# Attention tiles in slots, weight halves between the first loads, low parts from two products and an addition

## The chip, the cores and the metric

The kernel runs on one core of a Trainium2 chip. The core has a matrix engine (TensorE, PE in the profile), two engines for elementwise work (VectorE, DVE, and ScalarE, ACT), GpSimd (POOL) and a queue that issues DMAs (SyncE, SP). The metric is the device time of one execution in microseconds. Three runs of the kernel before took 1499.41, 1500.47 and 1502.14 us; the median is 1500.47.

## The reference

```python
# q, k, v: (8, 8, 576, 64) float32
q_c = q.reshape(B, H, nc, 64, D)           # chunks of 64 tokens, k_c and v_c alike
scores = scale * np.matmul(q_c, k_c.transpose(0, 1, 2, 4, 3))
attn = np.exp(scores - max); attn = attn / (sum(attn) + 1e-9)
x = matmul(attn, v_c) -> (4608, 512)       # tokens x (heads * 64)

h = x @ w_in                               # (512, 2048), float64 weights
g = np.maximum(h, 0.0) + np.log1p(np.exp(-np.abs(h)))     # softplus
x = (g @ w_out).astype(np.float32)         # (2048, 512)

h = np.maximum(np.maximum(x @ w1, x @ w2), x @ w3)        # 512 x 768 each
return (h @ w_out2).astype(np.float32)
```

The weights arrive as float64, so the chip reads each number as two 32-bit words.

## The kernel before

**Tiling.** The 4608 tokens are nine blocks of 512, each with four attention tiles (two heads of 512 tokens). The 2048 columns of the first MLP are 16 columns `j` of 128. For block `b` and column `j`, `mlp1` runs a projection group of twelve products (line 665, into a `ph` bank), softplus on ACT, a cut into a high and a low part, and a second group of twelve products (line 685) that adds into the four `acc` banks. After the last column of a block, four results are copied from `acc` to `tmp` tiles (lines 702 to 720) and stored to DRAM in `x2d`. The second MLP begins behind all of this and is not touched.

**Two parts.** Every operand of a product is held as a high part and a low part, and a product is three passes over them (`PASS`). `x` tiles and weight halves lie in slots of 128 x 2 x 512 numbers: 32 of kind `w`, 8 of kind `x`, 4 of kind `z`, one `qh`, one `vh`. Smaller results lie in nine `tmp` tiles (line 219). A buffer names its kinds in the order in which they are tried.

**Weights.** There are 32 weight halves (16 of `w_in`, 16 of `w_out`). `conv` loads one as pairs of words and turns it into a float `a` and a rest, in six DVE instructions (lines 301 to 339). `conv1` makes the two parts. For `j` under `SUMS` it copies `a` to the high part, lets PE sum `-high + a + rest` by three products with plus or minus the identity (lines 373 to 375), and ACT casts the sum to the low part. For the later `j`, `cut_up` does it on DVE with a subtraction and an addition.

**Attention.** The first eight tiles go through `attention_first`, with slots of kind `w`. The others go through `attention`: q and k are transposed on DVE into `tmp` tiles (lines 594, 595), PE makes the scores, softmax follows on DVE and ACT, the probabilities are transposed into a `tmp` tile (line 633), written to DRAM as `pd` and read back into another `tmp` tile by four DMAs (line 642). The products with v run with the next tile's scores (line 471).

**Early weights of the second MLP.** `early` converts 24 halves from block 2 on and stores them to DRAM; their slots are of kind `z`, then `x`.

**What sets the order.** `Plan.order` replays the kernel with costs and due times and gives each engine its list. An operation that allocates takes a free place at that moment; one that finds none waits, and others go first. On the chip each engine then runs its list in order and waits by semaphores; a tile that is used again waits for its last reader, a DMA store among them. SP's list holds nearly all loads and stores; ACT issues a part of the first ones.

Of the kernel before, what the change touches and what calls it, by code (L numbers as in the profile page):

```python
# [10 lines left out]
F32 = mybir.dt.float32  # L11
# [4 lines left out]
ALU = mybir.AluOpType  # L16
# [4 lines left out]
P = 128  # L21
# [157 lines left out]
def tile_kernel(ctx: ExitStack, tc: tile.TileContext, q, k, v, w_in, w_out, w1, w2, w3, wo2, out):  # L179
    nc = tc.nc  # L180
# [83 lines left out]
    T0, STEP = 30.0, 6.0  # L264
    T1 = T0 + STEP * (NB * NJ + 1)

    SUMS = 8
    turns = [(0, 0, 4), (1, 0, 8), (0, 4, NJ), (1, 8, NJ)]
    turns += [(b, 0, NJ) for b in range(2, NB)]
    steps = [(b, j, j == lo, j == hi - 1) for b, lo, hi in turns for j in range(lo, hi)]  # L270
# [6 lines left out]
    def in_line(kind, o):  # L277
        o.follow, line[kind] = line.get(kind), o
        return o


    def conv(src, view, kinds, due=None, after=(), most=("load",), rest=None):

        raw, a, t, free = slot(*kinds, shape=[P, TB, 2], dt=I32), Buf("tmp"), Buf("tmp"), Buf(*most)
        kind, j = view

        def load(e):
            if kind == "in":
                nc.sync.dma_start(
                    out=raw.t.rearrange("p (k f) t -> p k (f t)", k=KD),  # L290
                    in_=src[:, j * 2 * P:(j + 1) * 2 * P].rearrange("(k p) f -> p k f", p=P),
                )
            else:
                nc.sync.dma_start(out=raw.t.rearrange("p f t -> p (f t)"), in_=src[j * P:(j + 1) * P, :])

        in_line("load", op({"S": 0.5}, load, w=[raw], alloc=[free, raw], after=after, lat=2.0, move=2.2))
        hw = lambda: raw.t[:, :, 1]
        lw = lambda: raw.t[:, :, 0]
        ai = lambda: a.t.bitcast(I32)
        ti = lambda: t.t.bitcast(I32)  # L300
        op(
            {"D": 0.43},
            lambda e: nc.vector.tensor_scalar(ai(), hw(), 0x7FFFFFFF, None, ALU.bitwise_and),  # L303
            r=[raw],
            w=[a],
            alloc=[a, t],
        )
        op(
            {"D": 0.43},
            lambda e: nc.vector.tensor_scalar(  # L310
                a.t, a.t, f32_of_bits(0x47EFFFFF), f32_of_bits(0x38000000), ALU.min, ALU.max
            ),
            w=[a],
        )
        op(
            {"D": 0.43},
            lambda e: nc.vector.tensor_scalar(ai(), ai(), 3, 0x3FFFFFF8, ALU.logical_shift_left, ALU.bitwise_and),
            w=[a],
        )
        op(  # L320
            {"D": 0.69},
            lambda e: nc.vector.scalar_tensor_tensor(  # L322
                ai(), hw(), -0x40000000, ai(), ALU.bitwise_and, ALU.bitwise_or
            ),
            r=[raw],
            w=[a],
        )
        op({"D": 0.43}, lambda e: nc.vector.tensor_scalar(ti(), ai(), -0x800000, None, ALU.bitwise_and), r=[a], w=[t])
        last = op(
            {"D": 0.69},  # L330
            lambda e: nc.vector.scalar_tensor_tensor(
                rest.t[:, 1] if rest else t.t, lw().bitcast(U32), 2.0**-52, t.t, ALU.mult, ALU.mult
            ),
            r=[raw, t],
            w=[(rest, "rest")] if rest else [t],
            alloc=[rest] if rest else [],
            hold=[free],
            due=due,
        )
        return a, t, last  # L340
# [12 lines left out]
    def flat(z):  # L353
        return z.t if z.place[0] == "ph" else z.t[:, 0]
# [3 lines left out]

    def conv1(key, src, view, due):
        w = wbuf[key] = slot("w")  # L360
        kw = dict(most=("load", "load0"))
        if key[1] >= SUMS:
            a, t, last = conv(src, view, ("z", "w"), **kw)
            cut_up(w, lambda: a.t, [a], alloc=[w], rest=t, due=due)
            return last

        a, t, last = conv(src, view, ("z", "w"), rest=w, **kw)
        copy_op(lambda: w.t[:, 0], lambda: a.t, [a], [(w, "h")])
        ps = Buf("ph", "aps")

        def sums(e):
            o = flat(ps)
            nc.tensor.matmul(o, eye.t[:, 1, :P], w.t[:, 0], start=True, stop=False)  # L373
            nc.tensor.matmul(o, ident, a.t, start=False, stop=False)  # L374
            nc.tensor.matmul(o, eye.t[:, 0, :P], w.t[:, 1], start=False, stop=True)

        op({"P": 1.4}, sums, r=[eye, a, (w, "h"), (w, "rest")], w=[ps], alloc=[ps])
        copy_op(lambda: w.t[:, 1], lambda: flat(ps), [ps], [(w, "l")], psum=True, due=due, engs="A", after=[last])
        return last


# [200 lines left out]
        to_x(t, pv, view)  # L582

    before = []

    def attention(t, after=()):

        if t < NTILE:
            Rq, Rk, Rv = Buf("rq"), Buf("rk"), Buf("rv")
            qT, kT = Buf("tmp"), Buf("tmp")  # L590
            loads(load_32(t, q, lambda: Rq.t), Rq, "q", 2.2, [Rq], after=after)
            loads(load_32(t, k, lambda: Rk.t), Rk, "k", 2.2, [Rk], after=after)
            loads(load_v(t, lambda: Rv.t, 0), Rv, "v", 1.6, [Rv], after=after)
            op({"D": 0.69}, lambda e: nc.vector.transpose(qT.t, Rq.t), r=[Rq], w=[qT], alloc=[qT])
            op({"D": 0.69}, lambda e: nc.vector.transpose(kT.t, Rk.t), r=[Rk], w=[kT], alloc=[kT])
        G = Buf("aps")
        old = before.pop() if before else None

        def products(e):
            if old:  # L600
                v4 = old[1].t.rearrange("p (c e d) -> p c e d", e=2, d=D)
                p4 = old[2].t.rearrange("p (a u i) -> p u a i", a=2, i=32)
                for c in range(HP):
                    for r, k in four:
                        at = slice(TB // 2 + c * CH, TB // 2 + (c + 1) * CH)
                        square(G.t[:, :, at], v4[:, c, k], p4[:, k * HP + c], r, k)
            if t < NTILE:
                scores(G, lambda: qT.t, lambda: kT.t)

        parts = [(G, "v")] * (old is not None) + [(G, "s")] * (t < NTILE)  # L610
        op(
            {"P": 0.5 * len(parts) + 0.4},
            products,
            r=(list(old[1:]) if old else []) + ([qT, kT] if t < NTILE else []),
            w=parts,
            alloc=[G],
            after=last_t[-1:],
            due=T0 + STEP * (4 * (t - 1 - HP) + 2.25),
        )
        if old:  # L620

            def view(z, flat):
                if flat:
                    return z.rearrange("p (r f) -> p r f", r=2)
                return z[:, :, TB // 2:]

            to_x(old[0], G, view)
        if t == NTILE:
            return
        pbuf = Buf("p")  # L630
        softmax(G, pbuf)
        pt, pT = Buf("tmp"), Buf("tmp")
        op({"D": 0.69}, lambda e: nc.vector.transpose(
            pt.t.rearrange("p (b u i) -> p b u i", b=2, i=32), pbuf.t.rearrange("p (u b i) -> p b u i", b=2, i=32)
        ), r=[pbuf], w=[pt], alloc=[pt])
        pd = Buf("pd")
        op({"S": 0.48}, lambda e: nc.sync.dma_start(out=pd.t, in_=pt.t), r=[pt], w=[pd], alloc=[pd], lat=2.2)
        for n in range(4):
            c, b = divmod(n, 2)
            op(  # L640
                {"S": 0.48},
                lambda e, n=n, c=c, b=b: nc.sync.dma_start(
                    out=pT.t[n * 32:(n + 1) * 32, :].rearrange("j (a f) -> j a f", a=2),
                    in_=pd.t[c * CH:(c + 1) * CH, b * (TB // 2):(b + 1) * (TB // 2)].rearrange("(a j) f -> j a f", a=2),
                ),
                r=[pd],
                w=[(pT, n)],
                alloc=[pT] if n == 0 else [],
                lat=2.2,
            )  # L650
        before.append((t, Rv, pT))


    acc_of = {}
# [78 lines left out]
    def early(n, due, after):  # L733

        if n < NJ2:
            a, t, _ = conv(wo2, ("out", n), ("z", "x"), after=after)
            z = slot("z", "x")
            cut_up(z, lambda: a.t, [a], alloc=[z], rest=t, due=due)
            store["o", n] = op({"S": 0.48}, lambda e: nc.sync.dma_start(out=wo2d[n], in_=z.t.bitcast(F32)), r=[z], lat=2.0, move=2.2)
            return  # L740
        n -= NJ2
        a, t, _ = conv((w1, w2, w3)[n // 2 % 3], ("in", n // 6 * 2 + n % 2), ("z", "x"), after=after)
        tt_op(lambda: a.t, lambda: a.t, lambda: t.t, ALU.add, [t], [a], due=due)
        store["w", n] = op({"S": 0.48}, lambda e: nc.sync.dma_start(out=w2d[n], in_=a.t), r=[a], lat=2.0, move=1.1)

# [331 lines left out]
```

## Time and profile before

| | |
|---|---|
| median of three runs | 1500.47 us |
| profiled execution | 1499.52 us |
| its span in the profile | 1497.7 us |
| PE busy | 1445.6 us, 97% |
| DVE busy | 790.6 us, 53% |
| ACT busy | 456.5 us, 30% |

The trace is of one execution. A row of the order in time has a start, a duration, the engine, the line, the operation with output and inputs, and in brackets how long the engine had been idle and what ended that. PE's matmul durations overlap, so the distance between starts tells what one costs.

### The profile page before, as it was taken

The numbers are of one execution on the slowest core, as the hardware profiler recorded it, in microseconds if no ns is written. First come the engines' busy times: TensorE is split into PE (matmuls) and PEld (weight loads), VectorE is DVE, ScalarE is ACT, GpSimd is POOL, SyncE is SP. The second block draws the span as 40 slices with busy tenths as digits, with TensorE's granted clock in tenths as the row PEclk, the third lists the DMA queues.
The fourth block names the chain that finished last, engine by engine and source line by source line (L and its number), as shares of the span: only waits on it lengthen the run. The fifth ranks groups of instructions, "written<-read, shape, count | busy, mean of one in ns | idle before, by whom it ended". The sixth has DMA issues, their size and how long they took to land.

```text
span 1497.7 us, 26084 instructions
## 1 busy us (share of the span) xinstructions
PE 1445.6 (97%) x10642; PEld 1250.0 (83%) x10642; DVE 790.6 (53%) x1562; ACT 456.5 (30%) x890; POOL 0.7 (0%) x7
## 2 busy tenths in 40 slices
PE   4999999998998998989999999999999999999998
PEld 3677878887886886868888888999999999999997
DVE  6868874564443463535455355554554545545443
ACT  2533322232222132222222343332322323323222
POOL 0000000000000000000000000000000000000000
PEclk7999999999998999999999999999999999999999
DMA  7454235644424334343232321222322223222222
GB/s 248 135 144 138 86 83 130 152 127 112 115 59 117 88 81 119 83 99 100 63 127 65 112 64 36 92 71 85 99 85 86 74 82 105 80 85 86 70 71 85
DMA packets 229080, 147.48 MB, mean 98 GB/s; under 512 B 168032, under 2 KB 196704, under 8 KB 228960
## 3 DMA queue, kind: packets, MB, share of 16 engines
q1 hardware_dynamic: 225696, 144.24, 33.4%
q8 instruction: 83, 1.36, 0.4%
q10 hardware_dynamic: 3264, 1.57, 0.4%
q14 instruction: 37, 0.30, 0.1%
HBM read 109.58 MB, written 36.18 MB: 97 GB/s over the span
## 4 chain that ended last, share of the span: by engine, by line
PE 93%; DMA 2%; DVE 1%; SPq 1%; ACT 1%; issue 1%; ACTq 0%; DVEq 0%
PE acc L685 26%; PE ph L665 25%; PE ph L835 16%; PE one L835 12%; PE acc L953 10%; PE aps L471 2%; PE acc L471 1%; DMA x2d<-tmp 1%; PE ph L374 1%; DMA s<-in_q_dram 1%; SPq L438 1%; SPq L413 1%; ACT s L254 0%; PE ph L373 0%; ACT tmp L675 0%
## 5 line engine op out<-in xcount | busy, mean ns | idle before, releaser
L685 PE MATMUL acc<-g,s 128*128 128x512 f32 x1728 | 426.6, 396 | 18.4 <-ACT tmp L254 14.4
L665 PE MATMUL ph<-s,s 128*128 128x512 f32 x1728 | 418.1, 392 | 1.4 <-ACT tmp L675 1.4
L685 PEld LDWEIGHTS acc<-g,s 128*128 128x128 f32 x1728 | 326.1, 190 | 90.3 <-ACT tmp L254 15.9
L665 PEld LDWEIGHTS ph<-s,s 128*128 128x128 f32 x1728 | 325.8, 189 | 72.1 <-ACT tmp L675 2.4
L835 PE MATMUL ph<-s,s 128*128 128x256 f32 x1944 | 267.8, 283 | 0.0
L835 PEld LDWEIGHTS ph<-s,s 128*128 128x128 f32 x1944 | 251.8, 192 | 4.1
L261 DVE TENSOR_TENSOR tmp<-one,tmp 128x256 f32<-128x256 f32 x241 | 101.9, 423 | 246.9 <-PE one L835 217.3
L261 DVE TENSOR_TENSOR g<-tmp,g 128x512 fp32r<-128x512 f32 x198 | 135.9, 687 | 167.2 <-ACT g L254 163.1
L675 ACT ACTIVATE tmp<-ph 128x512 f32<-128x512 f32 x144 | 86.0, 598 | 426.1 <-PE ph L665 218.9
L254 ACT COPY tmp<-ph 128x256 f32<-128x256 f32 x268 | 100.2, 374 | 347.5 <-PE ph L835 346.3
L835 PE MATMUL one<-s,s 128*128 128x256 f32 x1458 | 201.6, 283 | 0.0
L835 PEld LDWEIGHTS one<-s,s 128*128 128x128 f32 x1458 | 186.7, 192 | 0.2
L953 PE MATMUL acc<-s,g 128*128 128x512 f32 x648 | 157.1, 391 | 0.5 <-DMA s<-wo2d 0.5
L953 PEld LDWEIGHTS acc<-s,g 128*128 128x128 f32 x648 | 118.3, 188 | 23.3 <-DMA s<-wo2d 0.9
L254 ACT CAST g<-tmp 128x512 fp32r<-128x512 f32 x191 | 119.1, 624 | 53.9 <-PE acc L685 40.0
L261 DVE TENSOR_TENSOR tmp<-tmp,tmp 128x256 f32<-128x256 f32 (+1 forms) x152 | 83.1, 547 | 3.9
L303 DVE TENSOR_SCALAR tmp<-s 128x512 int32<-128x512 int32 x56 | 23.5, 420 | 116.3 <-PE aps L471 107.0
L254 ACT CAST s<-tmp 128x512 fp32r<-128x512 f32 (+1 forms) x103 | 61.7, 604 | 27.9 <-DVE tmp L322 14.1
L254 ACT COPY tmp<-acc 128x512 f32<-128x512 f32 x48 | 27.7, 588 | 85.8 <-PE aps L471 27.2
L261 DVE TENSOR_TENSOR s<-tmp,s 128x512 fp32r<-128x512 f32 (+1 forms) x72 | 46.3, 654 | 7.5 <-ACT s L254 6.7
L256 DVE COPY tmp<-acc 128x512 f32<-128x512 f32 x17 | 11.8, 692 | 59.9 <-ACT tmp L254 39.8
L322 DVE SCALAR_TENSOR_TENSOR tmp<-s,tmp 128x512 int32<-128x512 int32 x56 | 38.3, 683 | 0.4
(85 smaller groups left out, 694.2 us busy)
## 6 DMA issues: line engine op xcount, KB each, us to landing
s<-wo2d SPq DMA_DIRECT2D x54, 512.0 KB, 3.3
s<-in_moe_w_out_dram SPq DMA_DIRECT2D x22, 512.0 KB, 4.7
x2d<-tmp SPq DMA_DIRECT2D x36, 256.0 KB, 2.7
s<-in_moe_w_dram SPq DMA_DIRECT2D x18, 512.0 KB, 3.9
s<-x2d SPq DMA_DIRECT2D x18, 512.0 KB, 4.8
s<-in_moe_w_in_dram SPq DMA_DIRECT2D x16, 512.0 KB, 5.0
out_dram<-tmp SPq DMA_DIRECT2D x29, 256.0 KB, 4.5
pd<-tmp SPq DMA_DIRECT2D x28, 256.0 KB, 2.0
```

Of the source, the lines that this page charges most:

```text
L254: nc.scalar.copy(dst(), src())
L261: return op({"D": 0.69 * n}, lambda e: nc.vector.tensor_tensor(dst(), a(), b(), f), r=r, w=w, **kw)
L303: lambda e: nc.vector.tensor_scalar(ai(), hw(), 0x7FFFFFFF, None, ALU.bitwise_and),
L322: lambda e: nc.vector.scalar_tensor_tensor(ai(), hw(), -0x40000000, ai(), ALU.bitwise_and, ALU.bitwise_or),
L374: nc.tensor.matmul(o, ident, a.t, start=False, stop=False)
L413: dma(out=dst().rearrange("p (g i) -> p g i", i=32)[a * 32:(a + 1) * 32, o // 32:(o + n) // 32, :], in_=src[b, t % HP * 2 + h, s:s + n, ha ...
L471: nc.tensor.matmul(dst[ROWS[k], r], w[ROWS[r]], x[ROWS[r]], start=True, stop=True)
L665: nc.tensor.matmul(ph.t, w[:, wi, kk * P:(kk + 1) * P], x[kk].t[:, xi], start=(kk == 0 and wi == 0 and xi == 0), stop=(kk == KD - 1 and wi ...
L675: in_line("y", op({"A": 0.6}, lambda e: nc.scalar.activation(l.t, ph.t, AF.Softplus), r=[ph], w=[l], alloc=[l]))
L685: nc.tensor.matmul(acc[m // 2].t[:, m % 2], w[:, wi, m * P:(m + 1) * P], g.t[:, gi, :], start=(first and wi == 0 and gi == 0), stop=(last ...
L835: nc.tensor.matmul(dst(), ws.t[:, wi, col + kk * P:col + (kk + 1) * P], x.t[:, xi, kk * HT:(kk + 1) * HT], start=(first and kk == 0 and wi ...
L953: nc.tensor.matmul(acc[t // 2].t[:, t % 2], g.t[:, gi, t * P:(t + 1) * P], wo.t[:, wi], start=(j == 0 and wi == 0 and gi == 0), stop=(j == ...
```

## The change

Four edits. The transposed q and k of an attention tile lie in the two halves of one slot (`qh`, then `z`), and the two tiles of transposed probabilities in another (`vh`, then `z`), in place of four `tmp` tiles. The first four weight halves get due times of their own for their loads (-70, -59, -55, -51), so that they stand between the first loads of q, k and v. `SUMS` is 16, so all 32 halves take the way over PE; PE now sums `rest - high` in two products, and DVE adds `a` while it writes the low part. `early` tries `x` before `z`, and raw weights of `j` from 12 on may only lie in `z`.

```diff
-    SUMS = 8
+    SUMS = 16
...
-        in_line("load", op({"S": 0.5}, load, w=[raw], alloc=[free, raw], after=after, lat=2.0, move=2.2))
+        in_line("load", op({"S": 0.5}, load, w=[raw], alloc=[free, raw], after=after, lat=2.0, move=2.2, due=first))
...
         w = wbuf[key] = slot("w")
-        kw = dict(most=("load", "load0"))
+        n = 2 * key[1] + key[2]
+        kw = dict(most=("load", "load0"), first=(-70.0, -59.0, -55.0, -51.0)[n] if n < 4 else None)
...
-        a, t, last = conv(src, view, ("z", "w"), rest=w, **kw)
+        a, t, last = conv(src, view, ("z", "w") if key[1] < 12 else ("z",), rest=w, **kw)
         copy_op(lambda: w.t[:, 0], lambda: a.t, [a], [(w, "h")])
         ps = Buf("ph", "aps")
 
         def sums(e):
             o = flat(ps)
-            nc.tensor.matmul(o, eye.t[:, 1, :P], w.t[:, 0], start=True, stop=False)
-            nc.tensor.matmul(o, ident, a.t, start=False, stop=False)
-            nc.tensor.matmul(o, eye.t[:, 0, :P], w.t[:, 1], start=False, stop=True)
-
-        op({"P": 1.4}, sums, r=[eye, a, (w, "h"), (w, "rest")], w=[ps], alloc=[ps])
-        copy_op(lambda: w.t[:, 1], lambda: flat(ps), [ps], [(w, "l")], psum=True, due=due, engs="A", after=[last])
+            nc.tensor.matmul(o, eye.t[:, 0, :P], w.t[:, 1], start=True, stop=False)
+            nc.tensor.matmul(o, eye.t[:, 1, :P], w.t[:, 0], start=False, stop=True)
+
+        op({"P": 0.5}, sums, r=[eye, (w, "h"), (w, "rest")], w=[ps], alloc=[ps])
+        tt_op(lambda: w.t[:, 1], lambda: flat(ps), lambda: a.t, ALU.add, [ps, a], [(w, "l")], due=due, after=[last])
...
-            qT, kT = Buf("tmp"), Buf("tmp")
+            QK = slot("qh", "z", dt=F32)
+            qT, kT = half(QK, 0), half(QK, 1)
...
-        pt, pT = Buf("tmp"), Buf("tmp")
+        PT = slot("vh", "z", dt=F32)
+        pt, pT = half(PT, 0), half(PT, 1)
...
-            a, t, _ = conv(wo2, ("out", n), ("z", "x"), after=after)
-            z = slot("z", "x")
+            a, t, _ = conv(wo2, ("out", n), ("x", "z"), after=after)
+            z = slot("x", "z")
...
-        a, t, _ = conv((w1, w2, w3)[n // 2 % 3], ("in", n // 6 * 2 + n % 2), ("z", "x"), after=after)
+        a, t, _ = conv((w1, w2, w3)[n // 2 % 3], ("in", n // 6 * 2 + n % 2), ("x", "z"), after=after)
```

The edits move instructions, because the order is planned from them. First ACT's list at the end of block 3 before: `ph` is a projection's bank, `acc` the banks of the second products, `g` their input, and the number behind `tmp` is the tile.

```order
L675 ACTIVATE tmp_75<-ph_90 128x512 [waits DVE_49,DMAHW2_49,PE_49,Activation_49]
L254 CAST g_74<-tmp_75 128x512 [waits Activation_49]
L254 COPY tmp_75<-acc_93 128x512 [waits DVE_49,PE_49]
L254 COPY tmp_75<-acc_93 128x512 [waits DMAHW0_49,Activation_49]
L254 COPY tmp_75<-acc_92 128x512 [waits DMAHW4_49,DMAHW3_49,DMAHW5_49,DMAHW2_49,DMAHW6_49,PE_49,Activation_49]
L675 ACTIVATE tmp_80<-ph_89 128x512 [waits PE_49]
```

The same place on ACT now (lines are two further down):

```order
L677 ACTIVATE tmp_82<-ph_90 128x512 [waits PE_49]
L254 CAST g_74<-tmp_82 128x512 [waits Activation_49]
L254 COPY tmp_78<-acc_93 128x512 [waits PE_49]
L254 COPY tmp_80<-acc_93 128x512 [waits DMAHW3_49]
L254 COPY tmp_75<-acc_92 128x512 [waits PE_49]
L254 COPY tmp_81<-acc_92 128x512
L677 ACTIVATE tmp_79<-ph_89 128x512 [waits DVE_49,PE_49]
```

Three of the copies went to one tile, the fourth to DVE; now four go to four tiles.

SP's list at the same block end before: `x2d` is the store of the copied results, `pd_87` the probabilities that are read back, `rv` the next v.

```order
L719 DMA x2d_123<-tmp_75 128x512 [waits DMAHW0_49,Activation_49]
L289 DMA s_125_4360<-in_moe_w_dram 128x4x256 [waits DMAHW1_49]
L719 DMA x2d_123<-tmp_75 128x512 [waits DMAHW2_49,Activation_49]
L642 DMA tmp_75<-pd_87 32x2x256 [waits DMAHW3_49,DMAHW2_49,PE_49]
L642 DMA tmp_75<-pd_87 32x2x256 [waits DMAHW4_49]
L642 DMA tmp_75<-pd_87 32x2x256 [waits DMAHW5_49,PE_49]
L642 DMA tmp_75<-pd_87 32x2x256 [waits DMAHW6_49]
L438 DMA rv_85<-in_v_dram 64x4x64 [waits DMAHW7_49,PE_49]
```

And now on SP:

```order
L645 DMA s_154_4314<-pd_87 32x2x256 [waits DMAHW7_49,DMAHW5_49]
L645 DMA s_154_4314<-pd_87 32x2x256 [waits DMAHW6_49]
L645 DMA s_154_4314<-pd_87 32x2x256
L645 DMA s_154_4314<-pd_87 32x2x256 [waits DMAHW0_49]
L289 DMA s_155_4356<-in_moe_w_dram 128x4x256 [waits DMAHW1_49,PE_49]
L413 DMA rk_84<-in_k_dram 32x4x32 [waits DMAHW2_49]
L413 DMA rk_84<-in_k_dram 32x4x32 [waits DMAHW3_49]
L721 DMA x2d_123<-tmp_78 128x512 [waits DMAHW4_49,Activation_49]
L721 DMA x2d_123<-tmp_80 128x512 [waits DMAHW5_49,Activation_49]
```

The four loads of probabilities stood behind two stores, and stand ahead of all four now.

PE's list up to the first projection product of the kernel before: `s_10` holds plus and minus the identity, `s_23`, `s_24`, `s_35` and `s_40` are the first block's `x`.

```order
L471 MATMUL acc_93<-s_39_777,s_28_555 64x64 [waits Activation_49]
L471 MATMUL acc_93<-s_39_777,s_28_555 64x64 x15
L373 MATMUL ph_89<-s_38_749,s_10_199 128x512
L374 MATMUL ph_89<-tmp_78,ident 128x512
L375 MATMUL ph_89<-s_38_749,s_10_199 128x512 [waits DVE_49]
L665 MATMUL ph_90<-s_23_502,s_13_262 128x512 x3
```

The same place on PE now: `s_4` is the identities, `s_22` holds q and k of the second block's first tile.

```order
L374 MATMUL ph_89<-s_40_713,s_4_191 128x512 [waits DVE_49]
L375 MATMUL ph_89<-s_40_713,s_4_191 128x512 [waits Activation_49]
L471 MATMUL acc_93<-ident,s_22_348 64x64 [waits DMAHW2_49,DMAHW1_49]
L471 MATMUL acc_93<-ident,s_22_348 64x64 x15
L471 MATMUL acc_93<-ident,s_22_348 64x64 [waits DMAHW4_49,DMAHW3_49]
L471 MATMUL acc_93<-ident,s_22_348 64x64 x15
L667 MATMUL ph_90<-s_33_532,s_15_235 128x512 x3
```

In both lists this sum is the fifth. Two turns of the second block's q and k with their scores came ahead of the projection before; one turn does now.

## Rows read from the trace of the kernel before

**Rows 1.** The page, first part: busy us, share of the span, instructions.

```profile
PE 1445.6 (97%) x10642; PEld 1250.0 (83%) x10642; DVE 790.6 (53%) x1562; ACT 456.5 (30%) x890; POOL 0.7 (0%) x7
```

**Rows 2.** Stretches: length, busy us (instructions) by engine, granted clock, DMA share, GB/s.

```profile
0.00:51.33 51.33, 30.18 (x852) 22.49 (x853) 32.74 (x73) 17.68 (x31) 0.74 (x7) 0.80 0.68 204
193.90:200.53 6.63, 4.60 (x14) 3.34 (x12) 6.63 (x14) 1.22 (x2) 0.00 (x0) 0.74 0.16 41
275.34:362.26 86.92, 86.92 (x617) 71.36 (x616) 49.25 (x91) 23.00 (x39) 0.00 (x0) 1.00 0.51 123
362.26:391.71 29.45, 25.08 (x161) 20.02 (x160) 13.43 (x23) 8.38 (x14) 0.00 (x0) 0.94 0.47 135
440.59:493.33 52.74, 46.96 (x309) 38.25 (x308) 20.11 (x37) 13.26 (x22) 0.00 (x0) 0.90 0.40 105
565.76:594.97 29.21, 22.57 (x149) 17.94 (x148) 12.04 (x22) 7.76 (x13) 0.00 (x0) 0.94 0.47 124
664.62:682.29 17.67, 11.91 (x102) 9.38 (x101) 10.71 (x19) 6.37 (x11) 0.00 (x0) 0.81 0.49 139
```

**Rows 3.** Order in time, 352 to 376: the end of block 2.

```profile
366.25 3.50 SPq L719 DMA_DIRECT2D x2d<-tmp  x4
...
368.82 0.59 ACT L254 COPY tmp<-acc 128x512 f32<-128x512 f32 x1 [1.73 <-DMA x2d<-tmp]
...
369.46 1.99 PE L685 MATMUL acc<-g,s 128*128 128x512 f32 x6 [3.35 <-ACT tmp L254]
...
371.25 4.21 PE L665 MATMUL ph<-s,s 128*128 128x512 f32 x12
```

**Rows 4.** Order in time, 448 to 478: the end of block 3.

```profile
463.65 0.59 ACT L254 COPY tmp<-acc 128x512 f32<-128x512 f32 x1 [4.92 <-DMA x2d<-tmp]
...
466.65 1.74 SPq L642 DMA_DIRECT2D tmp<-pd  x4
...
469.22 0.44 PE L471 MATMUL aps<-tmp,rv 64*64 64x64 f32 x2 [5.08 <-DMA tmp<-pd]
...
471.98 5.08 PE L685 MATMUL acc<-g,s 128*128 128x512 f32 x12
```

**Rows 5.** PE in order of time, 340 to 880: two more block ends.

```profile
575.52 2.93 PE L685 MATMUL acc<-g,s 128*128 128x512 f32 x6 [4.28 <-ACT tmp L254]
...
766.67 3.02 PE L685 MATMUL acc<-g,s 128*128 128x512 f32 x12 [0.29 <-ACT tmp L254]
```

**Rows 6.** PE in order of time, 0 to 200: a sum, and two groups.

```profile
116.95 0.40 PE L373 MATMUL ph<-s,s 128*128 128x512 f32 x1
...
118.28 2.91 PE L665 MATMUL ph<-s,s 128*128 128x512 f32 x12
...
131.89 2.88 PE L665 MATMUL ph<-s,s 128*128 128x512 f32 x12
134.61 2.88 PE L685 MATMUL acc<-g,s 128*128 128x512 f32 x12
```

**Rows 7.** Groups by line and form: busy us, mean ns, idle before.

```profile
L261 DVE TENSOR_TENSOR s<-aps,s 128x512 fp32r<-128x512 f32 x32 | 21.7, 677 | 1.3 <-ACT s L254 1.3
...
L254 ACT CAST s<-ph 128x512 fp32r<-128x512 f32 x14 | 8.2, 586 | 18.3 <-PE ph L375 15.9 <-DMA rq<-in_q_dram 2.0
```

**Rows 8.** ACT and DVE in order of time, 0 to 112: gaps in the front.

```profile
14.26 0.59 ACT L254 COPY s<-acc 128x512 f32<-128x512 f32 x1 [12.25 <-DMA s<-in_v_dram]
...
14.88 0.69 DVE L256 COPY s<-acc 128x512 f32<-128x512 f32 x1 [6.29 <-ACT s L254]
...
46.85 0.69 DVE L256 COPY s<-aps 128x512 f32<-128x512 f32 x1 [4.86 <-ACT s L254]
...
101.85 0.43 DVE L256 CAST g<-tmp 128x512 fp32r<-128x512 f32 x1 [6.11 <-ACT tmp L675]
```

**Rows 9.** PE in order of time, 0 to 200: the first projection group.

```profile
51.33 2.92 PE L665 MATMUL ph<-s,s 128*128 128x512 f32 x12
```

**Rows 10.** Who waited for whom: us in total, times, longest.

```profile
PE ph L373 <- ACT s L254: 2.4, 2, 1.2
```

More of the change, by code (lines that the diff above doesn't have):

```diff
@@ L279, in in_line, with conv @@
         return o
-    def conv(src, view, kinds, due=None, after=(), most=("load",), rest=None):
+    def conv(src, view, kinds, due=None, after=(), most=("load",), rest=None, first=None):
         raw, a, t, free = slot(*kinds, shape=[P, TB, 2], dt=I32), Buf("tmp"), Buf("tmp"), Buf(*most)
@@ L584, in tile_kernel @@
     before = []
+    half = lambda z, n: (lambda: z.t[:, n])
     def attention(t, after=()):
@@ L593, in attention @@
             loads(load_v(t, lambda: Rv.t, 0), Rv, "v", 1.6, [Rv], after=after)
-            op({"D": 0.69}, lambda e: nc.vector.transpose(qT.t, Rq.t), r=[Rq], w=[qT], alloc=[qT])
-            op({"D": 0.69}, lambda e: nc.vector.transpose(kT.t, Rk.t), r=[Rk], w=[kT], alloc=[kT])
+            op({"D": 0.69}, lambda e: nc.vector.transpose(qT(), Rq.t), r=[Rq], w=[(QK, "q")], alloc=[QK])
+            op({"D": 0.69}, lambda e: nc.vector.transpose(kT(), Rk.t), r=[Rk], w=[(QK, "k")])
         G = Buf("aps")
@@ L601, in products @@
                 v4 = old[1].t.rearrange("p (c e d) -> p c e d", e=2, d=D)
-                p4 = old[2].t.rearrange("p (a u i) -> p u a i", a=2, i=32)
+                p4 = old[2].t[:, 1].rearrange("p (a u i) -> p u a i", a=2, i=32)
                 for c in range(HP):
@@ L607, in products @@
             if t < NTILE:
-                scores(G, lambda: qT.t, lambda: kT.t)
+                scores(G, qT, kT)
         parts = [(G, "v")] * (old is not None) + [(G, "s")] * (t < NTILE)
@@ L613, in attention @@
             products,
-            r=(list(old[1:]) if old else []) + ([qT, kT] if t < NTILE else []),
+            r=([old[1]] + [(old[2], n) for n in range(4)] if old else []) + ([(QK, "q"), (QK, "k")] if t < NTILE else []),
             w=parts,
@@ L631, in attention @@
         softmax(G, pbuf)
-        pt, pT = Buf("tmp"), Buf("tmp")
+        PT = slot("vh", "z", dt=F32)
+        pt, pT = half(PT, 0), half(PT, 1)
         op({"D": 0.69}, lambda e: nc.vector.transpose(
-            pt.t.rearrange("p (b u i) -> p b u i", b=2, i=32), pbuf.t.rearrange("p (u b i) -> p b u i", b=2, i=32)
-        ), r=[pbuf], w=[pt], alloc=[pt])
+            pt().rearrange("p (b u i) -> p b u i", b=2, i=32), pbuf.t.rearrange("p (u b i) -> p b u i", b=2, i=32)
+        ), r=[pbuf], w=[(PT, "pt")], alloc=[PT])
         pd = Buf("pd")
-        op({"S": 0.48}, lambda e: nc.sync.dma_start(out=pd.t, in_=pt.t), r=[pt], w=[pd], alloc=[pd], lat=2.2)
+        op({"S": 0.48}, lambda e: nc.sync.dma_start(out=pd.t, in_=pt()), r=[(PT, "pt")], w=[pd], alloc=[pd], lat=2.2)
         for n in range(4):
@@ L642, in attention @@
                 lambda e, n=n, c=c, b=b: nc.sync.dma_start(
-                    out=pT.t[n * 32:(n + 1) * 32, :].rearrange("j (a f) -> j a f", a=2),
+                    out=pT()[n * 32:(n + 1) * 32, :].rearrange("j (a f) -> j a f", a=2),
                     in_=pd.t[c * CH:(c + 1) * CH, b * (TB // 2):(b + 1) * (TB // 2)].rearrange("(a j) f -> j a f", a=2),
@@ L646, in attention @@
                 r=[pd],
-                w=[(pT, n)],
-                alloc=[pT] if n == 0 else [],
+                w=[(PT, n)],
                 lat=2.2,
             )
-        before.append((t, Rv, pT))
+        before.append((t, Rv, PT))
     acc_of = {}
```

## The prediction

> **What bounds the kernel now.** I read the page's first part, then a table of stretches, then the order in time around the places where TensorE stands still. TensorE (PE) is busy for 97% of the span, VectorE (DVE) for 53%, ScalarE (ACT) for 30% [rows 1]. So the time is the work on PE plus the places where it waits, and a change gains only what it takes from one of these two.
>
> The waits are few. In the clean stretch from 275.34 to 362.26 PE is busy for all of 86.92 us at full clock [rows 2]. A projection group of twelve products takes 2.72 us (131.89 to 134.61 [rows 6]). The stretch holds 30 such groups and four attention pieces of 64 small products, so a piece costs (86.92 - 81.60) / 4 = 1.33 us. With these two prices the other stretches of rows 2 give what is lost at the ends of four token blocks; the groups follow from the instruction counts (161 is 64 + 8 x 12 and one more):
> 362.26 to 391.71: 29.45 - (8 x 2.72 + 1.33) = 6.36 us.
> 440.59 to 493.33: 52.74 - (15 x 2.72 + 2 x 1.33) = 9.28 us.
> 565.76 to 594.97: 29.21 - (7 x 2.72 + 1.33) = 8.84 us.
> 664.62 to 682.29: 17.67 - (3 x 2.72 + 1.33) = 8.18 us.
> Together 32.7 us. Part of it is the clock: it is granted at 0.81 to 0.94 there, and a group that follows a gap takes 4.21 or 5.08 us instead of 2.88 [rows 3, 4].
>
> The cause is a shortage of the nine `tmp` tiles. At 368.82 ACT's copy of a result from `acc` has waited until the store `x2d<-tmp` of its predecessor landed, and PE's next group waited 3.35 us for that copy [rows 3]. Before's order shows why: three of the four copies of a block end write the same tile, each behind the store of the one before. At 463.65 the copy waited 4.92 us for such a store. SP is in order, so the four loads of the transposed probabilities, issued at 466.65, stood behind a store that waited for this copy, and PE waited 5.08 us for them [rows 4]. The wait of 4.28 us at 575.52 is of the first kind [rows 5].
>
> The front has another limit. Until 51.33, the first projection product, PE is busy for 30.18 us at clock 0.80 [rows 2, 9], and DVE works through a chain with two long gaps: 6.29 us before 14.88 and 4.86 before 46.85 [rows 8].
>
> **The change part by part.**
> *Slots for the attention.* Four uses of `tmp` (q and k transposed, probabilities before and after the trip through DRAM) move to two slots, in `qh`, `vh` or `z`. The DVE and DMA instructions stay the same and cost nothing new. What goes is the reuse: after's order has four different tiles for the four copies, and no store before them in SP's queue waits for a copy that itself waits for a store. The block end at 766 shows what is left then, since before's order already has different tiles there: PE waits 0.29 us [rows 5]. ACT's four copies (2.4 us) lie under the group and the attention piece that PE runs between (2.72 + 1.33). Gain: 32.7 - 4 x 0.3 = 31.5 us. What is late next is ACT's softplus of the following column, with some 2 us to spare. Bounds: the two ends whose first wait was for `tmp<-pd` may keep theirs (18.1 us, if SP is late for another reason), or all 32.7 go.
>
> *The early block conversions* take slots of `x` before `z`. The next block's tiles also need `x`; nothing in the trace prices a wait for it. By the nearest rows it would be from zero to one gap of a block end, 9.3 us. I take zero: PE is the bound there, DVE was busy 49 of 87 us [rows 2], and after's order has the attention piece after every eighth group without exception.
>
> *Sums.* Before, a sum on PE takes 118.28 - 116.95 = 1.33 us, since the product with an unsplit fp32 operand costs several times the others [rows 6]. After, it is two products of 0.227 (2.72 / 12), 0.45 us. Now 32 halves of weights go this way rather than 16: 21.3 us of PE become 14.5. But in both orders five sums stand ahead of the first projection product, where PE isn't the bound. Behind it there are 11 x 1.33 = 14.6 before and 27 x 0.45 = 12.2 after: -2.4 us.
> On DVE each of the first 16 halves gains one addition that reads PSUM, 0.68 us by the like additions in rows 7 (10.8 us together), and each of the later 16 loses one subtraction of the same length. ACT loses 16 casts of 0.59 [rows 7], work off the path.
> Whether DVE's extra 10.8 us show depends on who leads. I counted both orders with the trace's durations. DVE's work up to the last `x` tile of the first block is 35.5 us before and 33.7 after; up to that of the second block 69.8 and 72.4. PE's work between the first products of these two blocks is 35.0 and 36.5. So at the second block DVE is later by (72.4 - 33.7) - (69.8 - 35.5) = 4.4, of which PE has 1.5 to fill. Beyond it the shares turn: at the last weights, where PE waited for DVE before and lost 6.63 - 2.72 = 3.9 us [rows 2], DVE has some 16 us in hand by the same count.
>
> The Trainium skill speaks against this part: "VectorE: DVE Perf Modes", Specifications, has ScalarE as the engine nearer to PSUM and VectorE as the one nearer to SBUF, and the change takes PSUM reads from ACT to DVE. The trace agrees in size (0.59 against 0.68 us). By the rule, with DVE as the bound, the front would be longer by the whole 10.8 us; that is the first rival.
>
> *Loads.* Four weight halves (0.5 MB each) go between the first q, k and v. Before, ACT issued loads until it could start its first copy at 14.26, waiting 12.25 us [rows 8]. In after's order ACT issues the same twelve loads, and the data ahead of its last one is about as much (three weight halves come in, most of v falls behind), so I keep 14 to 16 us. DVE gets a second half to convert in its gap of 6.29: I take 2 us less idle. If the v loads are late instead, the first tile starts up to 4 us later (1.5 MB more at the 204 GB/s of this stretch [rows 2] would be 7 us, half of it under DVE's conversions).
> *Waits of the sums themselves.* A sum can stop PE where its inputs come late. Before, the 16 sums did so twice, for 2.4 us [rows 10]; for 27 I take 27 / 16 x 2.4 = 4.1, with bounds of 0 and the 10.8 us above.
>
> Sum of the front: -2.4 (sums) - 3.9 (the wait at 196) - 2 (loads) + 2.9 (second block) + 4.1 = -1.3 us. Bounds: -8.3 (only the gains) and +10.8.
>
> **Sum.** 1497.7 - 31.5 - 1.3 = 1464.9 us of span. The profiled execution took 1499.52, 1.8 more than its span, and the median of the runs is 0.95 above it: 1464.9 + 1.8 + 0.95 = 1468 us. From the last attention piece on, PE's order is the same in both kernels, and its time stays.
>
> **Rivals.**
> *VectorE bounds the front.* For it: it is busy 32.74 of the first 51.33 us, with gaps only where others wait [rows 2, 8]. Against: the later halves return the work, and it idled 6.11 us before 101.85 until ACT's softplus came [rows 8]. Time: 1468 + 1.3 + 10.8 = 1480. Chance 0.11.
> *SP, not `tmp`, holds the probabilities.* The loads of v behind them wait for PE, and SP is in order. The ends at 469 and 566 keep their losses: 1468 + 18 = 1486. Against it: after's order has those loads ahead of the block's stores. Chance 0.09.
> *Slower: sums hold the PSUM banks.* `ph` has two banks, shared by projections and sums. Before, ACT, which is idle 70% of the time, emptied them; after, DVE does, behind up to a whole conversion (with the addition seven instructions of 0.43 or 0.69 us, as those in rows 8, some 3.8 us). Each of 27 sums that holds PE for more than (31.5 + 1.3) / 27 = 1.2 us makes the kernel slower; at 1.5 us it is 1468 + 40 = 1508. Against it: between a sum and the next projection into its bank there is mostly a group of 2.72 us. Chance 0.05.
> *No effect*: the stalls come back with other tiles, 1500. Chance 0.03.
>
> **How the numbers follow.** The forecast, 1461 to 1475 by its own terms, has 0.72. The range 1457 to 1488 takes in the first two rivals and leaves out the last two and the tails. Faster by over 0.2% (3 us, about what a measurement of this kernel can tell from no change): 0.92; within it 0.03; slower 0.05.
>
> **What would show it.** In the changed kernel PE should have no wait for ACT's copies of over 1 us at the block ends, none for the probabilities, a clock of 1.0 from some 60 us on, and 92 us for each block of 16 columns. The first projection product should start between 48 and 54 us. A first product past 58, or PE waiting for DVE again and again between 55 and 200, speaks for the first or third rival. I would be wrong altogether if PE waited at a block's first projection for a tile of `x`.

## The result and the profile after

The changed kernel takes 1463.03 us (median of 4 runs, 1461.89 to 1463.24), the kernel before 1499.94 beside it (1498.55 to 1502.14): a ratio of 0.9751, 95% interval 0.9734 to 0.9768. The forecast was 1468 in a range of 1457 to 1488. The profiled run has a span of 1461.2 us, 36.5 less than before.

The first part of the page after (busy us, share of the span, instructions), against [rows 1]:

```profile
PE 1430.9 (98%) x10642; PEld 1245.2 (85%) x10642; DVE 786.1 (54%) x1551; ACT 454.2 (31%) x885; POOL 0.7 (0%) x7
```

Stretches of the changed kernel, with the columns of [rows 2]; the last one runs from the attention piece at 290.40 to the last piece:

```profile
0.00:45.64 45.64, 25.86 (x715) 20.48 (x715) 32.76 (x73) 15.21 (x26) 0.73 (x7) 0.89 0.77 230
193.90:200.53 6.63, 6.63 (x89) 5.34 (x88) 3.58 (x7) 1.80 (x3) 0.00 (x0) 1.00 0.72 190
261.66:290.40 28.74, 24.75 (x161) 20.11 (x161) 19.89 (x37) 7.33 (x12) 0.00 (x0) 0.94 0.60 153
290.40:798.16 507.76, 507.76 (x3521) 417.33 (x3520) 251.96 (x460) 146.81 (x242) 0.00 (x0) 1.00 0.39 101
```

And the same stretch of the kernel before:

```profile
298.47:834.82 536.35, 512.91 (x3498) 419.10 (x3497) 253.67 (x466) 140.86 (x234) 0.00 (x0) 0.98 0.36 95
```

In the changed kernel TensorE is busy for all of 507.76 us, at full clock; its 22 attention pieces come every 23.08 us, which is eight groups and a piece, 8 x 2.72 + 1.33. The stretch of before holds 23 instructions fewer, which is two groups of 2.72 us (24, with one record missing). Without waits it would take 507.76 - 5.44 = 502.32 us, so it lost 34.0.

The end of block 2 after, in order of time on ScalarE; it answers to [rows 3]:

```profile
355.67 1.07 ACT L254 COPY tmp<-acc 128x512 f32<-128x512 f32 x2
357.03 1.07 ACT L254 COPY tmp<-acc 128x512 f32<-128x512 f32 x2 [0.28 <-PE acc L687]
359.75 0.60 ACT L677 ACTIVATE tmp<-ph 128x512 f32<-128x512 f32 x1 [1.64 <-PE ph L667]
```

Four copies in two pairs, and the only thing they wait for is TensorE.

One wait is new. In order of time on VectorE and TensorE, at the end of block 1:

```profile
264.12 0.43 DVE L303 TENSOR_SCALAR tmp<-s 128x512 int32<-128x512 int32 x1 [4.65 <-DMA s<-in_moe_w_out_dram]
264.46 0.68 DVE L261 TENSOR_TENSOR g<-tmp,g 128x512 fp32r<-128x512 f32 x1
265.06 0.42 DVE L310 TENSOR_SCALAR tmp<-tmp 128x512 f32<-128x512 f32 x1
265.40 2.47 DVE L261 TENSOR_TENSOR tmp<-acc,tmp 128x512 f32<-128x512 f32 x4
...
266.82 4.57 PE L687 MATMUL acc<-g,s 128*128 128x512 f32 x12 [3.99 <-DVE tmp L261]
```

VectorE works its list in order. It stands 4.65 us for the load of the first early weight, which SP issued at 259.50, and behind that conversion stand the four additions of the parked partial sums, which TensorE needs before it may write the next block's `acc`. The stretch is 28.74 us instead of 23.08: 5.66 lost, 3.99 as a wait and the rest at the lower clock after it (4.57 us for a group of 2.88). A second profile of the same kernel (a2_after_again below) has 2.86 us of this wait and 4.53 lost.

Where the 36.5 us are: 5.7 ahead of the first projection product (45.64 against 51.33 [rows 9]), 2.6 between it and 290 without the new wait, less 5.7 by the new wait, 34.0 behind, and -0.2 after the last piece. The 2.6 is what is left: the place that has as much work behind it as 298.47 of before is 290.40 + 5.44 = 295.84, which is 2.63 us earlier, and -5.69 + 5.66 - 2.6 gives that. The 5.7 is not all gain, since less work stands ahead of the product (715 instructions against 852 in the first stretches): 128 small products of the second block's q and k stand behind it now, and 128 of them take 2.0 us there (49.09 to 51.07).

### The profile page after: what moved, and what is told of

It reads as the page before. It is cut to its first block, busy times and chain, and to the rows that moved or that the text cites. A ratio compares the mean times of both kernels' runs of the same rounds, so it can differ in the third digit from the quotient of the medians.

```text
span 1461.2 us, 25970 instructions
## 1 busy us (share of the span) xinstructions
PE 1430.9 (98%) x10642; PEld 1245.2 (85%) x10642; DVE 786.1 (54%) x1551; ACT 454.2 (31%) x885; POOL 0.7 (0%) x7
## 4 chain that ended last, share of the span: by engine, by line
PE 96%; DMA 2%; DVE 1%; ACT 0%; issue 0%; SPq 0%; ACTq 0%; DVEq 0%
PE acc L687 27%; PE ph L667 27%; PE ph L837 16%; PE one L837 12%; PE acc L955 10%; PE aps L471 2%; PE acc L471 1%; DMA s<-in_moe_w_out_dram 1%; PE ph L374 1%; PE ph L375 0%; ACT s L254 0%; DMA s<-in_k_dram 0%; DMA pd<-s 0%; DMA s<-wo2d 0%; DVE tmp L261 0%
## 5 line engine op out<-in xcount | busy, mean ns | idle before, releaser
L687 PE MATMUL acc<-g,s 128*128 128x512 f32 x1728 | 420.8, 393 | 4.0 <-DVE tmp L261 4.0
L596 DVE STREAM_TRANSPOSE s<-rq 128x512 f32<-128x512 f32 x28 | 19.9, 710 | 64.7 <-PE aps L471 45.8
```

The source lines that it names most:

```text
L596: op({"D": 0.69}, lambda e: nc.vector.transpose(qT(), Rq.t), r=[Rq], w=[(QK, "q")], alloc=[QK])
L687: nc.tensor.matmul(acc[m // 2].t[:, m % 2], w[:, wi, m * P:(m + 1) * P], g.t[:, gi, :], start=(first and wi == 0 and gi == 0), stop=(last ...
```

## Experiments

**The slots alone.** The kernel before, with `attention` alone taken from the changed one:

```diff
-            qT, kT = Buf("tmp"), Buf("tmp")
+            QK = slot("qh", "z", dt=F32)
+            qT, kT = half(QK, 0), half(QK, 1)
-        pt, pT = Buf("tmp"), Buf("tmp")
+        PT = slot("vh", "z", dt=F32)
+        pt, pT = half(PT, 0), half(PT, 1)
```

> The kernel before with one part of the change alone: the attention's transposed tiles lie in slots (sums, loads, early conversions as before). Tile theory: the four block ends lost 32.7 us because nine tmp tiles were shared by the attention and the accumulator copies; with the attention out of them the four copies of a block end find four tiles, no wait of TensorE for a ScalarE copy above 1 us is left after 300 us, and the time is 1464 to 1472 us. Rival, the order theory: the waits went because the sixteen sums and the earlier loads moved the copies and the stores, so slots alone give less than half, 1480 to 1497 us.

Measured 1466.5 us, ratio 0.9785 (0.9763 to 0.9807). Its stretches:

```profile
264.01:292.74 28.73, 24.75 (x162) 20.13 (x161) 19.71 (x37) 7.33 (x12) 0.00 (x0) 0.94 0.61 163
292.74:800.50 507.76, 507.76 (x3521) 417.23 (x3520) 253.40 (x462) 146.56 (x242) 0.00 (x0) 1.00 0.39 101
```

The slots alone take away the whole loss behind 290 us, and they are enough to bring the new wait at the end of block 1. The order theory falls.

**Everything but the slots.** The changed kernel with `attention` of before and `SUMS = 8`.

> The changed kernel without the slots: the attention's transposed tiles are back in the nine tmp tiles, and the sums cover eight columns as before (in their new form); the first loads and the early conversions stay as changed. Tile theory: the block ends lose 25 to 37 us again, with copies of one block end that share a tile, and the time is 1485 to 1498 us. Order theory: the block ends stay quiet, under 1472 us.

Measured 1483.11 us, 0.9894 (0.9875 to 0.9914), a little under the expected 1485. TensorE's waits in it (us in all, times, longest):

```profile
PE acc L685 <- ACT tmp L254: 12.0, 4, 4.4
...
PE aps L471 <- DMA tmp<-pd: 5.1, 2, 4.7
```

And the stretch from 288.08 to its last piece:

```profile
288.08:818.29 530.21, 509.80 (x3497) 417.10 (x3496) 254.33 (x469) 139.10 (x232) 0.00 (x0) 0.99 0.37 96
```

530.21 - 502.32 = 27.9 us lost, inside the 25 to 37 expected, with the two kinds of wait of [rows 3, 4].

**The copies in slots, the attention left alone.** The kernel before, but at the ends of blocks 2 to 8 the four copies go elsewhere:

```diff
+            if b >= 2:
+                if m % 2 == 0:
+                    both = slot("qh", "vh", "x", dt=F32)
+                at = lambda both=both, m=m: both.t[:, m % 2]
...
+                continue
             o = Buf("tmp")
```

> The kernel before, its attention left in the nine tmp tiles as it was, but the four accumulator copies at the ends of blocks 2 to 8 go into halves of two slots that lie free there. Tile theory: whichever user leaves the nine tiles, the shortage goes; no copy waits for a store, the losses of 32.7 us go, 1464 to 1475 us. Rival, the probabilities theory: what TensorE waited for at a block's end was the attention's chain through SP's queue, which holds its tile loads in order whatever the copies do; then at least half of the loss stays, 1482 to 1500 us.

Measured 1467.44 us, 0.9791 (0.9772 to 0.981). The attention goes through `tmp`, DRAM and SP's queue as before, and yet the losses go:

```profile
297.85:804.29 506.44, 503.32 (x3498) 412.71 (x3497) 250.44 (x462) 142.71 (x239) 0.00 (x0) 1.00 0.39 101
```

Only 506.44 - 502.32 = 4.1 us stay, most of them ten waits of 0.30 or 0.35 us for ScalarE's softplus. Copies and attention took the same tiles from each other; whichever goes, the waits go. The probabilities theory (my second rival) falls.

**Five tiles instead of nine.** `mem("tmp", 9, ...)` becomes `mem("tmp", 5, ...)` in the changed kernel.

> The changed kernel with five tmp tiles instead of nine. The attention took up to four of the nine before, so five is what it left. Count theory: five tiles run as short as nine did with the attention among them, block ends lose about 30 us, 1488 to 1500 us. Holding theory: it was not the count, but that the attention's tiles are held across the way to DRAM and back (pd) and across SP's queue; with users that hold a tile for 1 to 3 us, five do nearly as well as nine, 1461 to 1472 us.

Measured 1468.0 us, 0.9795 (0.9777 to 0.9814). Around the end of block 2 it loses 1.5 us, and from 387.61 on nothing is lost:

```profile
187.00:250.24 63.24, 58.11 (x367) 46.09 (x365) 39.54 (x74) 17.98 (x30) 0.00 (x0) 1.00 0.45 109
387.61:803.04 415.43, 415.43 (x2881) 341.36 (x2880) 202.24 (x372) 115.90 (x191) 0.00 (x0) 1.00 0.35 93
```

18 pieces in 415.43 us are 23.08 each. It pays ahead of that, 5.1 us of it as waits of TensorE in 187 to 250, where the weights' conversions want two tiles each. It pays more than the 5 us by which the kernel is slower, because the new wait at block 1's end isn't in this run. So five tiles are enough for the later block ends once the attention is out.

That does not speak against a shortage in number, because the attention left fewer than five. The expectation took it to hold up to four of the nine; the trace of before shows more. Each of the 28 attention tiles there transposes q once and k once and has one group of scores, all in the same order, so counting tells which belongs to which (VectorE and TensorE: the 13th q, and the 10th and the 13th scores):

```profile
343.14 0.71 DVE L594 STREAM_TRANSPOSE tmp<-rq 128x512 f32<-128x512 f32 x1 [6.03 <-DMA rk<-in_k_dram]
...
362.78 0.65 PE L471 MATMUL aps<-tmp,tmp 64*64 64x64 f32 x32
...
441.11 0.65 PE L471 MATMUL aps<-tmp,tmp 64*64 64x64 f32 x32
```

The q transposed at 343.14 is held until 441.11, 98 us. When the copies of block 2 wait at 366, 13 q and 13 k have been transposed and the scores of 10 tiles have run: six of the nine `tmp` tiles are held. It is eight (17, 17 and 13) at 463, five at 570 and six at 668, the other ends that lose over 6 us, and four at 766, where 0.35 us was lost. The probabilities held a tile too, for 10.5 us at a time (SP and TensorE):

```profile
311.06 0.32 SPq L642 DMA_DIRECT2D tmp<-pd  x1
...
321.55 0.69 PE L471 MATMUL aps<-tmp,rv 64*64 64x64 f32 x32
```

So the attention ran several tiles ahead and left one to four for everything else. How many are held does not decide alone: in the run without slots an end with six (749 us) lost 0.35. No run varied the holding by itself, or tried more than nine tiles.

**Eight and twelve columns of sums.** `SUMS = 8` and `SUMS = 12` in the changed kernel.

> The changed kernel with the sums on TensorE for eight columns of weights instead of sixteen (two products and one addition each, as changed). If the front gained its 9.5 us by the new form of the sums and the loads, eight columns do as well: 1459 to 1465 us, with the sums' 16 x 0.45 us gone from TensorE and the same 16 products' worth of VectorE work back. If the gain came from taking VectorE work away in columns 8 to 15 (the wait of 3.9 us at 196 us of the kernel before), that wait is back: 1466 to 1470 us.

> The changed kernel with sums on TensorE for twelve columns of weights instead of sixteen. TensorE saves 8 x 0.45 = 3.6 us. Theory: VectorE takes the work of eight halves back without making TensorE wait more than 1 us in all, 1458 to 1461 us. Rival: waits for VectorE return as they did with eight columns (2.5 and 3.3 us at 178 and 188 us), and it comes out even, 1461 to 1465 us.

Measured 1460.37 us with eight (0.9735, 0.971 to 0.976) and 1463.19 with twelve (0.9758, 0.9736 to 0.978). The three intervals overlap: the number of columns can't be told apart by time. Twelve misses the 1458 to 1461 of its theory and falls to its rival: TensorE waits 3.14 us for VectorE at 189.41. Eight, in order of time on TensorE:

```profile
177.71 4.38 PE L687 MATMUL acc<-g,s 128*128 128x512 f32 x11 [2.46 <-DVE g L261]
...
188.34 4.38 PE L687 MATMUL acc<-g,s 128*128 128x512 f32 x11 [3.31 <-DVE g L261]
```

With eight, TensorE waits for VectorE again, though its time is no worse: the 16 sums that it leaves out (7.2 us of TensorE) about pay for them. Waits came back, as the second theory said, but its time of 1466 to 1470 didn't.

**The old form of the sums.** All sixteen columns with three products and a copy:

```diff
-            nc.tensor.matmul(o, eye.t[:, 0, :P], w.t[:, 1], start=True, stop=False)
-            nc.tensor.matmul(o, eye.t[:, 1, :P], w.t[:, 0], start=False, stop=True)
+            nc.tensor.matmul(o, eye.t[:, 1, :P], w.t[:, 0], start=True, stop=False)
+            nc.tensor.matmul(o, ident, a.t, start=False, stop=False)
+            nc.tensor.matmul(o, eye.t[:, 0, :P], w.t[:, 1], start=False, stop=True)
...
-        tt_op(lambda: w.t[:, 1], lambda: flat(ps), lambda: a.t, ALU.add, [ps, a], [(w, "l")], due=due, after=[last])
+        copy_op(lambda: w.t[:, 1], lambda: flat(ps), [ps], [(w, "l")], psum=True, due=due, engs="A", after=[last])
```

> The changed kernel with the old form of the sums for all sixteen columns: three products (one of them on whole fp32 numbers) and a ScalarE copy in place of two products and a VectorE addition. Price theory: a sum costs TensorE 1.33 us instead of 0.45 us, 27 of the 32 stand behind the first projection product, so about 24 us more on a TensorE that is never idle there, less some VectorE time: 1478 to 1490 us. Rival: the sums lie in waits that TensorE has anyway in the first 200 us, under 1470 us.

Measured 1484.8 us, 0.9905 (0.9884 to 0.9926): 21.8 more than the changed kernel, near the 24 expected. A sum in the old form, in order of time on TensorE:

```profile
108.56 0.40 PE L374 MATMUL ph<-s,s 128*128 128x512 f32 x1
108.80 1.02 PE L375 MATMUL ph<-tmp,ident 128*128 128x512 f32 x2
109.26 0.80 PE L376 MATMUL ph<-s,s 128*128 128x512 f32 x1
109.89 2.91 PE L668 MATMUL ph<-s,s 128*128 128x512 f32 x12
```

And one in the new form, from the changed kernel:

```profile
99.81 0.39 PE L374 MATMUL ph<-s,s 128*128 128x512 f32 x1
100.03 0.39 PE L375 MATMUL ph<-s,s 128*128 128x512 f32 x1
100.26 2.88 PE L667 MATMUL ph<-s,s 128*128 128x512 f32 x12
```

1.33 us against 0.45, or 27 x 0.88 = 23.8 us behind the first projection product, and the price is paid in full, since TensorE hardly waits there. That the time came so near the 24 expected is in part luck: here the first projection product comes 1.6 us later (47.28), and the new wait at block 1's end, 5.7 us in the changed kernel, isn't there. Moving the third term of the sum to VectorE was right even though VectorE reads PSUM for it.

**Without the early loads.** `first=None` in place of the four due times.

> The changed kernel without the due times that put four weight halves between the first loads of q, k and v; all else as changed. Loads theory (the prediction's): they bring the front 2 us, so 1464 to 1466 us here, the first projection product 1 to 3 us later than 45.64 us. Rival: they are the whole of the front's gain, then the first projection product comes at 48.5 us or later and the time is 1466 to 1470 us. Other rival: VectorE, busy with conversions it gets sooner, is what the first columns wait for anyway, and nothing changes, 1462 to 1464 us.

Measured 1460.84 us, 0.9747 (0.9727 to 0.9768): not slower. The first projection product does come later:

```profile
49.41 3.02 PE L667 MATMUL ph<-s,s 128*128 128x512 f32 x12
```

That is 3.8 us after the changed kernel's, but with 872 instructions ahead of it instead of 715. At the piece near 239 us only 1.0 is left of it (239.60 against 238.58), and then the planner's other order happens to shrink the new wait: the pieces that start at 262.68, 309.38 and 333.52 take 0.54, 1.06 and 0.66 us longer than 23.08, 2.3 in all against 5.66. The expected mechanism was seen at 45 us and not in the time.

**The early conversions' slots.** `("z", "x")` again in place of `("x", "z")`.

> The changed kernel with the early conversions taking a z slot before an x slot, as in the kernel before. The prediction put this edit at nothing (bound 0 to 9.3 us): 1461 to 1465 us, attention pieces 23.08 us apart. Rival: z slots that the transposed tiles now share with the conversions run short, and pieces after 290 us stand apart by more than 24 us: 1467 to 1473 us.

Measured 1462.66 us, 0.9758 (0.9738 to 0.9777), with the changed kernel at 1462.87 beside it: nothing, as the prediction had it.

**The additions first.** The changed kernel with two dependences more, where `adds[4:]` are block 1's four additions:

```diff
-            alloc=[a, t],
+            alloc=[a, t], after=behind,
...
-        a, t, _ = conv(wo2, ("out", n), ("x", "z"), after=after)
+        a, t, _ = conv(wo2, ("out", n), ("x", "z"), after=after, behind=() if n else adds[4:])
...
-            op({"D": 0.69}, lambda e: nc.vector.transpose(qT(), Rq.t), r=[Rq], w=[(QK, "q")], alloc=[QK])
-            op({"D": 0.69}, lambda e: nc.vector.transpose(qT(), Rq.t), r=[Rq], w=[(QK, "q")], alloc=[QK])
+            op({"D": 0.69}, lambda e: nc.vector.transpose(qT(), Rq.t), r=[Rq], w=[(QK, "q")], alloc=[QK], after=adds[4:] if t == 13 else ())
```

> The changed kernel with two added dependences: the first conversion step of the first early weight, and the transposes of one q, k tile, come behind the four additions of block 1's parked partial sums on VectorE. Queue theory: the one wait left after 60 us (3.99 us at 266.82, a stretch of 28.74 us instead of 23.08) is VectorE standing for a weight's load with the additions behind it; with the additions ahead it goes, 1456.5 to 1459.5 us. Rival, the drain theory: a block's last accumulator is free only some 4 us after its last product whatever VectorE does first, and the wait stays or another takes its place (tile of x, probabilities), 1461 to 1465 us.

> The kernel with the additions ahead once more, on one chip with the changed kernel. If the wait at block 1's end was worth its stretch, the difference to the changed kernel is -0.25 to -0.5% here too (5.4 us at 1457.6 against 1463.0 us, read on two chips); if that was the difference of two chips, it is under 0.1%.

> The changed kernel itself, for comparison on one chip: 1461 to 1465 us.

Measured 1457.59 us (0.9726, 0.9706 to 0.9747), and beside the changed kernel on one chip 1456.59 (1455.16 to 1459.35) against 1462.87 (1462.68 to 1463.35): the runs don't overlap, and the medians differ by 0.43%. In order of time on VectorE and TensorE in the run of this pair:

```profile
256.05 2.48 DVE L261 TENSOR_TENSOR tmp<-acc,tmp 128x512 f32<-128x512 f32 x4
256.68 5.60 PE L667 MATMUL ph<-s,s 128*128 128x512 f32 x24
...
259.07 0.38 DVE L303 TENSOR_SCALAR tmp<-s 128x512 int32<-128x512 int32 x1
...
263.30 3.02 PE L687 MATMUL acc<-g,s 128*128 128x512 f32 x12
```

And the stretch after the block's end, between two pieces:

```profile
262.21:282.57 20.36, 20.36 (x149) 16.71 (x149) 14.82 (x29) 5.99 (x10) 0.00 (x0) 1.00 0.51 128
```

The additions run while TensorE works on two projection groups, and the group that needs them doesn't wait: 20.36 us is seven groups and a piece, 7 x 2.72 + 1.33. The queue theory holds, and this version beats both kernels. Not all of the difference is the wait's, though. The spans of the two profiled runs of the pair differ by 7.7 us. 4.5 of it is the stretch at block 1's end in a2 (262.67 to 290.28, 27.61 us instead of 23.08). The other 3.2 lie ahead of the piece at 239.59 (236.41 here), where TensorE's rows come in the same order in both.

## Why the prediction was right, and where it was off

*Block ends* (31.5 us forecast). Right in place and cause; 34.0 came. The residual of 0.3 at each end isn't there, and before also lost 0.4 in each of two stretches between the ends (from 524.57 and 620.77) and 0.35 at 766. "A shortage of the nine tiles" has to be put more exactly: at the four ends five to eight of them lay with q and k transposed far ahead, and five would do once the attention is out.

*"What is late next".* This step failed. I named ScalarE's softplus, and looked for new waits only at the ends of blocks 2 and later. What came was VectorE's wait for a weight at the end of block 1, 5.7 us. With the slots the planner puts a conversion ahead of the four additions, and its load came at 264.12, after TensorE had run out of other work at about 262.8. How much that costs goes with the order: TensorE waits 3.98 us with the slots alone, 2.45 with twelve columns, 0.47 without the early loads, and not at all with the old sums or five tiles.

*Sums.* The price of 0.45 us was right. "The waits of the sums themselves" (+4.1) was too dear: behind the first projection product one of 0.78 us came. The two waits of [rows 10] from which it was scaled lie at 33.60 and 43.48, ahead of that product, and did not belong in a count of what comes behind it. The second block's lag (+2.9) was 1.4: from the first projection product of the first block to that of the second it is 37.79 us after (45.64 to 83.43) and 36.36 before (51.33 to 87.69). The second one after:

```profile
83.43 8.38 PE L667 MATMUL ph<-s,s 128*128 128x512 f32 x36
```

And before:

```profile
87.69 5.60 PE L665 MATMUL ph<-s,s 128*128 128x512 f32 x24
```

The mechanism of this lag was wrong as well: VectorE was to be the late one, but TensorE is busy for 37.39 of the 37.79 us. The lag is TensorE's own work, the 128 small products more, and near the 1.5 us of the forecast's count for TensorE. That 1.4 already holds the sums of this stretch, three before and six after, which -2.4 counts too (3 x 1.33 - 6 x 0.45 = 1.3). Counted once, -2.4 + 1.3 - 3.9 + 1.4 + 0.8 is -2.8 for what lies behind the first projection product; the trace has -2.6. The wait of 3.9 at 196 went, but more than one part can take it away: with the slots alone it is down to 0.65 us, at 192.05; with the slots and the new sums in eight columns such waits are back (2.46 and 3.31), and sixteen columns take them off.

*Loads* (-2). Without them the first projection product comes 3.8 us later, the piece at 239 us 1.0 later, and the whole kernel takes no more time. That product came at 45.64, outside the 48 to 54 I had named; the forecast left out that less work stands ahead of it.

*Sum.* 1464.9 us of span were forecast and 1461.2 came: the front and the block ends together gained 9.4 us more than I had, and the new wait took 5.7 back. The 3.7 us between them are the difference of two larger errors, so that the number came this close is luck; that the block ends give most of it is not.

*Rivals.* VectorE didn't bound the front: between 55 and 200 us TensorE waited for it twice, for 0.8 and 0.5 us, and the granted clock was 1.00 from 50 us on until the new wait. The Trainium skill ("VectorE: DVE Perf Modes", Specifications) has VectorE as the engine farther from PSUM. The trace agrees in sign: the same copy out of `acc` takes 0.69 us on VectorE and 0.59 on ScalarE [rows 8]. VectorE had the time, so nothing came of it here. The slower rival (sums that hold PSUM banks) would have shown as waits of TensorE for VectorE's additions at the sums or at the projections behind them; these two of 0.8 and 0.5 us are all there are behind the first projection product.

## What to carry to other kernels

Where copies wait for the stores of their predecessors, ask who else holds tiles of that pool, how many at once and for how long: here one user had run ahead and held up to eight of nine. Moving either user out took all or nearly all of the loss, and five tiles were enough for the others from block 3 on. More tiles were not tried. After a stall is taken out, go through each in-order engine of the new order for an instruction that waits for a load and has an accumulator's reader behind it. A stall can cost more than its wait: 3.99 us of waiting cost 5.66 here, since the clock was low for the group after it, while with twelve columns 2.45 us at the same place cost 2.51 and the group after it took 3.00.

## What was not expected of the hardware

The clock in the front differs from run to run. The kernel with the slots alone and the kernel before run the same groups up to there, but the first projection product came at 48.85 in one and 51.33 in the other. A sum in the kernel before, in order of time on TensorE:

```profile
39.36 0.79 PE L373 MATMUL ph<-s,s 128*128 128x512 f32 x1
39.95 1.91 PE L374 MATMUL ph<-tmp,ident 128*128 128x512 f32 x2
```

And the same sum with the slots alone:

```profile
38.43 0.50 PE L373 MATMUL ph<-s,s 128*128 128x512 f32 x1
38.77 1.02 PE L374 MATMUL ph<-tmp,ident 128*128 128x512 f32 x2
```

The one pays the 1.2 GHz price for it (granted clock 0.57 from this sum to the next), the other that of 2.4 GHz (1.00). A third profile of this order, that of the copies in slots, pays the 1.2 GHz price too and has the product at 50.85. So three profiles of one order spread over 2.5 us, and up to 2.5 of the 5.7 us that the front seemed to gain may be the clock; no term of a front should be read from one profile to better than that.
